# Identity products in TensorE's gaps, an earlier second batch and other tile addresses in a fused Nyström attention and gated MLP on one Trainium2 core

## The chip, the cores and the metric

One Trainium2 chip, one core of it. The metric is device microseconds of one execution of the whole program, the median of several runs; lower is better. TensorE's clock is granted at one of two levels, 1.2 GHz and 2.4 GHz; the profile gives the granted clock of a stretch as a share of 2.4 GHz (0.50 and 1.00). Engines: PE is TensorE, PEld its weight loads, DVE VectorE, ACT ScalarE, POOL GpSimd, SP the engine whose queue issues the transfers.

## The reference

```python
def _attn_ref(q, k, v):                  # 8 batches, 8 heads, 576 tokens, 64 wide
    m, scale = 32, 1.0 / np.sqrt(D)
    q_lm = q.reshape(B, H, m, S // m, D).mean(axis=3)      # 32 landmarks of 18 tokens
    k_lm = k.reshape(B, H, m, S // m, D).mean(axis=3)
    A  = sm(q, k_lm)                      # sm: softmax of scale * a @ b.T
    Bm = sm(q_lm, k_lm)
    C  = sm(q_lm, k)
    Z = Bm.T / (norm1(Bm) * norminf(Bm) + 1e-06)
    for _ in range(6):
        Z = 2 * Z - Z @ Bm @ Z
    return A @ Z @ C @ v

def _moe_ref(x, w_gate, w_val, w_out, rms_g):   # x: 4608 tokens x 512
    rms = np.sqrt(np.mean(x * x, axis=-1, keepdims=True) + 1e-06)
    xn = x / rms * rms_g
    g, val = xn @ w_gate, xn @ w_val            # 512 x 1536 each
    return (silu(g) * val) @ w_out              # 1536 x 512
```

q and k are drawn 8 times as large as standard normals times 0.1. The inputs are float64 in memory; the kernel reads them as pairs of 32-bit words.

## The kernel before

**The attention of a batch b** goes through these steps. `sums` adds 18 tokens to a landmark (DVE, tile `lmT`). `front(b, g)`, for each half g of the heads, makes the scores `sC` and `sA` (16 products of 288 columns and 4 of 32), takes maxima (`mx`, DVE), exponentials (`E`, `eb`, ACT) and transposes `sA` to `tA` (DVE). `turn` transposes `E` on TensorE (`sE`, `sF`), `values` makes `pCV`. Then comes the inverse: `newton_start`, `newton_first` (`p`) and six `newton_step`s, each of 8 small products (`pn`, 32 rows x 32 columns of the array; two records each in the profile) and one DVE instruction (`PV`, at the last step `VF`) which the next step waits for. `newton_weights` makes `W` (`pW`, 8 small products, then a copy) and `newton_values` transposes it to `WT` (`pT`). `second(b)` makes the attention's output `pO` in two sets of four banks, squares it on ACT (`sq`), adds the squares up (`pss`, `pms`), and takes 1/rms by a chain of small DVE instructions (`ms`, `r`); with that it scales `AT` and casts it into `an`, the left operand of everything that follows. The scores, `pO`, `pss`, `pn`, `pW` share four PSUM banks (pool `pa`); `pM`, `psg`, `psv` and `pso` share four others (`pg`).

**The MLP.** The attention's output is never formed: `mix_weights` multiplies the weights of a pair of feature tiles by `WT` (`pM`, cast into `Mhi` and `Mlo`), and `psg` and `psv` (6 products of 288 columns each, four such pairs of groups for each feature tile pair) come out of `Mhi`, `Mlo` and `an`. `s` is silu(gate) times value, `h` its high and low part, and `pso` (`whio`, `wloo`: 3 products for each of 6 feature tiles and each tile of 128 tokens) is the output. The first 6 feature tiles go over all 8 batches and leave partial sums; then the other 6 (`lhio`, `lloo`, `lgv`, `anl`, `obl`) go over them again.

**Weights** come in as pairs of words (`wrawg`, `wrawv`, `wrawo`) and are put together on chip: for each gate or value tile ACT runs two instructions of 128x512 (L175, L178), DVE two (L180, L183), into `wgv`, one such tile for a pair of feature tiles, with four pieces in it. Nine raw tiles are fetched ahead, the later ones when a place in the ring comes free.

**The order of work** on each engine is the order in which the program issues it. A `Mixer` takes pieces from several generators; `until(c, n)` lets a generator wait until the MLP has issued n pieces of chunk c (a chunk is a batch of the first or the second half). In the first 100 us, before the MLP runs without holes, the order is: batch 0's scores and inverse, `second(0)` with `pM` of the first pair in it, then `front(1, 0)`, the first `psg` and `psv`, and `pM` of the second pair, which needs the four pieces of the second `wgv` tile. `early.stream` issues the putting together of weights, `early.then` and `early.after` say behind which instruction.

**Addresses.** A tile's start in each partition comes from the order of allocation. Before, `gsb` (16 bytes) leaves all tiles allocated behind it on the left side (`WT`, `h`, `whio`, `wloo`, `Mhi`, `Mlo`, `an`, `s`, the raw weights, `qk`, `lhio6`, `lgv3`) at 32 bytes past a multiple of 64; those of the right side (`AT`, `sq`, `lhio7` to `lhio11` and `lloo7` to `lloo11`, `lgv4`, `lgv5`, `obl`) start at multiples of 64.

Of the kernel before, what the change touches and what calls it, by code (L numbers as in the profile page):

```python
# [19 lines left out]
P = 128  # L20
M = 32
# [34 lines left out]
def nystrom_moe_kernel(  # L56
# [25 lines left out]
    RS = 0.375**2  # L82
# [19 lines left out]
    gsb = cst.tile([P, NK], F32, name="gsb")  # L102
    WT = cst.tile([P, B, NK, 2 * M], F32, name="WT")

# [21 lines left out]
    class Weights:  # L126

        def __init__(self, order, place, spots, ahead=0):
            self.order, self.queue = list(order), list(order)
            self.place = place  # L130
            self.spots, self.ahead, self.after, self.then = spots, ahead, None, None
            self.raws, self.gv, self.out = {}, {}, {}
# [22 lines left out]
        def load_next(self):  # L155
# [27 lines left out]
            nc.vector.scalar_tensor_tensor(  # L183
                w, whead, -0x80000000, w, op0=ALU.bitwise_and, op1=ALU.bitwise_or
            )
            if nm == "o":
# [95 lines left out]
    def mlp(wts, b, f0, an, store, part, following):  # L282
# [4 lines left out]
        for n, pair in enumerate(pairs):  # L287
# [5 lines left out]
            for i in range(2):  # L293
                if very and i and n + 1 < NPAIR:
                    mix_weights(wts, b, pairs[n + 1])
                    yield 1.1
                s = mp.tile([P, S], F32, name="s", tag="s", bufs=2)
                for e in range(2):
                    cols = slice(e * HS, (e + 1) * HS)
# [56 lines left out]
    with tc.tile_pool(name="ap", bufs=1, side="right") as ap, tc.tile_pool(  # L356
# [30 lines left out]
        def front(b, g, after=None):  # L387
# [59 lines left out]
            if b:  # L447
                tail(after)
# [25 lines left out]
        def turn(b, g):  # L474
# [4 lines left out]
            sF = pa.tile([2 * M, P], F32, name="sF", tag="pa")  # L479
            tp(sF, E[:, 4 * P :], ident)  # L480
            ET = ap.tile([P, 4, P], F32, name="ET", tag="ET", bufs=1)
# [7 lines left out]
        def values(b, g):  # L489
# [3 lines left out]
            pCV = pa.tile([P, D], F32, name="pCV", tag="pa")  # L493
            for ch in range(5):
                for h in range(4):
# [7 lines left out]
                    )  # L503
            nc.vector.tensor_scalar_mul(nt["PV"][:, g, M:], pCV, nt["rs"][g][:, 0:1])

        def opening():
# [18 lines left out]
        def rest(b, inverse, at):  # L525
# [26 lines left out]
            with tc.high_priority():  # L552
                newton_weights(b, inverse[2])
            yield 0.4, 0.0
            yield from until(*next(at))
            with tc.high_priority():
                newton_values(b)
            yield 0.3, 0.0
# [10 lines left out]
        def steady():  # L569
            n_gv = NF1 * 24  # L570
            yield 0.0, TW
            new_state(1)
            sums(1, 0)
            while stage["second"] < 0:
                yield -0.3
            front(1, 0, fixed["an", 0].ins)
            load_qk(2, 0)
            yield 1.3, 0.0
            sums(1, 1, fixed["mx", 1, 0].ins)
            yield from until(0, 24)  # L580
            turn(1, 0)
            yield 0.65, 0.0
            yield from until(0, 36)
# [375 lines left out]
```

## Time and profile before

| | |
|---|---|
| median of 3 runs | 837.14 us (836.75 to 837.6) |
| the profiled execution | 836.84 us, of which the span is 834.7 us |
| TensorE busy | 800.4 us, 96% of the span |
| DVE, ACT, POOL busy | 490.9, 350.9, 71.0 us |
| mean granted clock | 0.973 |
| chain that ended last | 86% of the span on TensorE |

The span is the time from the first to the last instruction; 2.1 us of the execution lie outside it. An engine's busy time is the union of its instructions' spans. Idle time before an instruction is put down to what released it, with an arrow. A product of two fp32 operands stands as two records in the trace, so "x16" for `pn` is 8 products.

### The profile page before, as it was taken

The numbers are of one execution on the slowest core, as the hardware profiler recorded it, in microseconds if no ns is written. First come the engines' busy times: TensorE is split into PE (matmuls) and PEld (weight loads), VectorE is DVE, ScalarE is ACT, GpSimd is POOL, SyncE is SP. The second block draws the span as 40 slices with busy tenths as digits, with TensorE's granted clock in tenths as the row PEclk, the third lists the DMA queues.
The fourth block names the chain that finished last, engine by engine and source line by source line (L and its number), as shares of the span: only waits on it lengthen the run. The fifth ranks groups of instructions, "written<-read, shape, count | busy, mean of one in ns | idle before, by whom it ended". The sixth has DMA issues, their size and how long they took to land.

```text
span 834.7 us, 17401 instructions
## 1 busy us (share of the span) xinstructions
PE 800.4 (96%) x7192; PEld 630.3 (76%) x7192; DVE 490.9 (59%) x1095; ACT 350.9 (42%) x749; POOL 71.0 (9%) x97
## 2 busy tenths in 40 slices
PE   7756999999999999999999999999999999999998
PEld 4334667877878778777787879797979797979796
DVE  7787976856768748668584945242524252425241
ACT  4557644535445444445464844141414141414140
POOL 1012411020020200201110110000000000000000
PEclk8579999999999999999999999999999999999999
DMA  9756452250440612503436510413141304130202
GB/s 326 242 172 216 143 191 89 84 195 15 144 136 2 228 65 92 188 2 109 140 114 229 176 71 13 145 54 118 22 146 53 121 22 147 50 124 14 88 14 75
DMA packets 41054, 95.49 MB, mean 114 GB/s; under 512 B 4112, under 2 KB 17424, under 8 KB 38928
## 3 DMA queue, kind: packets, MB, share of 16 engines
q1 hardware_dynamic: 40976, 94.39, 33.4%
q8 instruction: 56, 0.92, 0.5%
q14 instruction: 22, 0.18, 0.1%
HBM read 66.06 MB, written 28.31 MB: 113 GB/s over the span
## 4 chain that ended last, share of the span: by engine, by line
PE 86%; DVE 5%; DMA 4%; ACT 2%; POOL 1%; issue 1%; SPq 1%; ACTq 0%; DVEq 0%
PE pso L109 35%; PE psg L109 19%; PE psv L109 18%; PE pM L109 6%; PE pn L109 2%; DMA wrawg<-in_moe_w_gate_dram 2%; PE pO L109 1%; PE sC L109 1%; PE pss L109 1%; DMA wrawv<-in_moe_w_val_dram 1%; PE pCV L109 1%; DMA qk<-in_k_dram 1%; PE sE L112 1%; DVE wgv L180 1%; SPq L152 0%
## 5 line engine op out<-in xcount | busy, mean ns | idle before, releaser
L109 PE MATMUL pso<-whio,h 128*128 128x512 f32 x432 | 140.7, 397 | 2.1 <-ACT ob L848 2.1
L109 PE MATMUL pso<-lhio,h 128*128 128x512 f32 x432 | 138.7, 396 | 0.0
L316 DVE TENSOR_TENSOR s<-s,psv 128x288 f32<-128x288 f32 x192 | 85.9, 450 | 60.0 <-PE psv L109 59.3
L315 ACT ACTIVATE s<-psg 128x288 f32<-128x288 f32 x192 | 78.7, 410 | 89.9 <-PE psg L109 89.5
L268 ACT CAST Mhi<-pM 128x512 fp32r<-128x512 f32 x96 | 51.4, 591 | 137.6 <-PE pM L109 137.2
L323 ACT CAST h<-s 128x576 fp32r<-128x576 f32 x96 | 64.6, 673 | 86.2 <-DVE s L316 86.2
L109 PEld LDWEIGHTS pso<-whio,h 128*128 128x128 f32 x432 | 81.6, 189 | 24.3 <-issue 4.2
L109 PEld LDWEIGHTS pso<-lhio,h 128*128 128x128 f32 x432 | 81.0, 187 | 24.8 <-DVE obl L911 5.9
L324 DVE TENSOR_TENSOR h<-s,h 128x576 fp32r<-128x576 f32 x96 | 72.7, 758 | 44.5 <-ACT h L323 44.3
L109 PE MATMUL psg<-an,Mhi 128*128 128x288 f32 x384 | 85.4, 307 | 4.8 <-ACT s L315 3.4
L911 DVE TENSOR_TENSOR obl<-obl,pso 128x512 f32<-128x512 f32 x36 | 24.8, 688 | 107.6 <-PE pso L109 107.4
L109 PE MATMUL pso<-wloo,h 128*128 128x512 f32 x216 | 86.4, 400 | 0.0
L109 PE MATMUL pso<-lloo,h 128*128 128x512 f32 x216 | 85.2, 395 | 0.0
L109 PE MATMUL psv<-an,Mhi 128*128 128x288 f32 x384 | 84.4, 303 | 0.0
L270 DVE TENSOR_TENSOR Mlo<-pM,Mhi 128x512 fp32r<-128x512 f32 x94 | 60.3, 683 | 37.5 <-ACT Mhi L268 37.5
L109 PE MATMUL psg<-anl,Mhi 128*128 128x288 f32 x384 | 81.7, 301 | 0.6 <-DVE Mlo L270 0.6
L109 PE MATMUL psv<-anl,Mhi 128*128 128x288 f32 x384 | 79.1, 294 | 0.0
L109 PEld LDWEIGHTS psg<-an,Mhi 128*128 128x128 f32 x384 | 62.3, 191 | 17.5 <-issue 6.7
L109 PEld LDWEIGHTS psg<-anl,Mhi 128*128 128x128 f32 x384 | 60.9, 188 | 15.5 <-issue 12.6
L109 PEld LDWEIGHTS psv<-an,Mhi 128*128 128x128 f32 x384 | 61.6, 188 | 6.1 <-issue 2.2
L109 PEld LDWEIGHTS psv<-anl,Mhi 128*128 128x128 f32 x384 | 61.5, 188 | 0.0
L109 PE MATMUL psg<-an,Mlo 128*128 128x288 f32 x192 | 58.5, 305 | 0.0
(138 smaller groups left out, 1249.8 us busy)
## 6 DMA issues: line engine op xcount, KB each, us to landing
qk<-in_q_dram SPq DMA_DIRECT2D x16, 576.0 KB, 4.8
qk<-in_k_dram SPq DMA_DIRECT2D x16, 576.0 KB, 5.8
ad<-an SPq DMA_DIRECT2D x8, 1152.0 KB, 5.1
pd<-ob SPq DMA_DIRECT2D x36, 256.0 KB, 2.4
anl<-ad SPq DMA_DIRECT2D x8, 1152.0 KB, 5.1
obl<-pd SPq DMA_DIRECT2D x36, 256.0 KB, 2.7
out_dram<-obl SPq DMA_DIRECT2D x36, 256.0 KB, 2.0
vt<-in_v_dram SPq DMA_DIRECT2D x16, 512.0 KB, 4.1
```

Source lines behind the costliest of these rows:

```text
L109: tc.keep_in_program_order(nc.tensor.matmul(*args, **kw))
L112: tc.keep_in_program_order(nc.tensor.transpose(*args))
L180: nc.vector.scalar_tensor_tensor(w, w, 3, wtail, op0=ALU.logical_shift_left, op1=ALU.bitwise_or)
L268: nc.scalar.copy(hi[:, g], ps[g])
L270: nc.vector.tensor_sub(lo[:, g], ps[g], hi[:, g].bitcast(F32))
L315: silu["last"] = nc.scalar.activation(s[:, cols], banks[0], AF.Silu).ins
L316: nc.vector.tensor_mul(s[:, cols], s[:, cols], banks[1])
L323: nc.scalar.copy(h[:, 0, TAIL:], s)
L324: gated[b, f0 // NF1, 2 * n + i] = nc.vector.tensor_sub(h[:, 1, TAIL:], s, h[:, 0, TAIL:].bitcast(F32))
L911: nc.vector.tensor_add(ob, ob, ps)
```

## The change

Seven things are done at once.
- **Identity products** (`idle`, `spare`): in batch 0's inverse TensorE multiplies the identity by itself, into a bank that nobody reads: 4 products behind the first `turn`, 1 behind the first `values`, 4 behind `p`, 2 behind each of the six `pn`, 1 behind `pW`; 22 in all.
- **`newton_weights`** makes `W` and its transpose at once from a matrix `blocks` (128 x 2 x 128, zero outside its blocks; GpSimd copies `Bs` into it) by 2 full products of 64 columns and 2 of 128 in place of 8 small ones and two transposes. `VF` is written twice by two DVE instructions. `newton_values` is gone, and with it one stop of the stream for each batch.
- **`front(1, 0)`** and the landmark sums that it needs stand behind `pO` of batch 0 instead of behind `an`; `pms` comes ahead of `pM`.
- **Putting weights together**: ACT's part of the ninth tile stands ahead of the eight squares instead of between them, DVE's part of the fifth ahead of `mx`; the rest follows `an` directly. `sums(1, 1)` moves behind it.
- **1/rms** takes 7 instructions of 128x18 behind `ms` instead of 10.
- **`pM` of the next pair** in the very first chunk comes one group of 12 products later; `front(1, 1)` and batch 1's inverse get other places.
- **Addresses**: `gsb` takes 64 bytes, so the tiles of the left side start at multiples of 64 as well; `rT` shares the place of `sqT`.

```diff
-    RS = 0.375**2
+    RS = 0.375
...
-    gsb = cst.tile([P, NK], F32, name="gsb")
+    gsb = cst.tile([P, 16], F32, name="gsb")[:, :NK]
...
+    blocks = cst.tile([P, 2, P], F32, name="blocks")
+    nc.gpsimd.memset(blocks, 0.0)
...
             for i in range(2):
-                if very and i and n + 1 < NPAIR:
-                    mix_weights(wts, b, pairs[n + 1])
-                    yield 1.1
                 s = mp.tile([P, S], F32, name="s", tag="s", bufs=2)
                 for e in range(2):
+                    if very and i and e and n + 1 < NPAIR:
+                        mix_weights(wts, b, pairs[n + 1])
+                        yield 1.1
...
+        def idle(out, n):
+
+            for _ in range(n):
+                mm(out, ident, ident, start=True, stop=True)
+
+        def spare(n):
+            idle(pg.tile([P, 512], F32, name="psw", tag="pg")[:, :P], n)
...
             for g in range(2):
-                turn(0, g)
+                turn(0, g, 4 - 4 * g)
...
-                values(0, g)
+                values(0, g, 1 - g)
...
-            yield 0.0, TW
-            new_state(1)
-            sums(1, 0)
             while stage["second"] < 0:
                 yield -0.3
-            front(1, 0, fixed["an", 0].ins)
-            load_qk(2, 0)
-            yield 1.3, 0.0
-            sums(1, 1, fixed["mx", 1, 0].ins)
-            yield from until(0, 24)
+            yield from until(0, 12)
             turn(1, 0)
             yield 0.65, 0.0
-            yield from until(0, 36)
+            yield from until(0, 37)
+            sums(1, 1, early.last)
+            yield from until(0, 46)
             front(1, 1)
...
-            at = [46, 58, 70] + [78 + 8 * n for n in range(6)] + [126, 132, 138, n_gv + 4, n_gv + 10, n_gv + 18]
+            at = [54, 66, 78] + [84 + 7 * n for n in range(6)] + [126, 136, n_gv + 4, n_gv + 10, n_gv + 18]
...
-                after = [7 * n for n in range(7)] + [48, 54, 68, 86, 96]
+                after = [7 * n for n in range(6)] + [48, 56, 68, 86, 96]
...
+            for h in range(4):
+                nc.gpsimd.tensor_copy(blocks[rows(h), :, rows(h ^ 1)], Bs[rows(h)])
...
-                nt["VF"] = to = sm.tile([P, 2, D], F32, name="VF", tag="VF", bufs=1)
-                of = PV[:, :, M:]
+                nt["VF"] = sm.tile([P, 2, 2, D], F32, name="VF", tag="VF", bufs=1)
+                for g in range(2):
+                    of, by = (a[:, g].unsqueeze(1).broadcast_to([P, 2, D]) for a in (PV[:, :, M:], pn))
+                    nc.vector.scalar_tensor_tensor(nt["VF"][:, g], of, 2.0, by, op0=ALU.mult, op1=ALU.subtract)
+                return
...
-                for h in range(4):
-                    r = rows(rho(g, h))
-                    mm(pW[rows(pos(g, h)), g], Bs[r, g, :], VF[r, g, :], start=True, stop=True)
-            W = sm.tile([P, 2, 2, D], F32, name="W", tag="W", bufs=2)
-            fixed[b] = nc.vector.tensor_copy(W, pW.unsqueeze(2).broadcast_to([P, 2, 2, D]))
+                mm(straight[:, g], blocks[:, g], VF[:, g, 0], start=True, stop=True)
+            for g in range(2):
+                mm(turned[:, g], VF[:, g].rearrange("p a d -> p (a d)"), blocks[:, g], start=True, stop=True)
+            W = sm.tile([P, 2, D], F32, name="W", tag="W", bufs=2)
+            fixed[b] = nc.vector.tensor_copy(W, straight)
...
             newton_first(b, *inverse)
             early.then = fixed["PV", b].ins
+            spare(4)
...
                 newton_step(b, n)
+                spare(2)
                 yield 0.45, NP
-            newton_weights(b, inverse[2])
-            yield 0.4, WW
-            newton_values(b)
-            yield 0.3, WW
+            newton_weights(b)
+            spare(1)
+            yield 0.6, WW
...
-            nc.vector.tensor_single_scalar(ri, ms.bitcast(I32), 1, op=ALU.logical_shift_right)
-            nc.vector.tensor_scalar(ri, ri, -1, 0x5F3759DF, op0=ALU.mult, op1=ALU.add)
-            for c in (1.0, RS):
-                nc.vector.tensor_mul(r2, r1, r1)
-                nc.vector.scalar_tensor_tensor(r2, r2, c, ms, op0=ALU.mult, op1=ALU.mult)
-                nc.vector.scalar_tensor_tensor(r2, r2, -10.0 / 3.0, r2, op0=ALU.add, op1=ALU.mult)
-                last = nc.vector.scalar_tensor_tensor(r1, r2, 5.0, r1, op0=ALU.add, op1=ALU.mult)
+            nc.vector.tensor_scalar(
+                r1.bitcast(I32), ms.bitcast(I32), -0.5, 0x5F3759DF, op0=ALU.mult, op1=ALU.add
+            )
+            nc.vector.tensor_mul(r2, r1, r1)
+            nc.vector.scalar_tensor_tensor(r2, r2, -0.5, ms, op0=ALU.mult, op1=ALU.mult)
+            nc.vector.scalar_tensor_tensor(r1, r2, 1.5, r1, op0=ALU.add, op1=ALU.mult)
+            nc.vector.tensor_mul(r2, r1, r1)
+            nc.vector.tensor_mul(r2, r2, ms)
+            nc.vector.scalar_tensor_tensor(r2, r2, -10.0 / 3.0, r2, op0=ALU.add, op1=ALU.mult)
+            last = nc.vector.scalar_tensor_tensor(r1, r2, 5.0, r1, op0=ALU.add, op1=ALU.mult)
...
-            rT = ap.tile([P, S], F32, name="rT", tag="rT", bufs=1)
+            rT = ap.tile([P, S], F32, name="rT", tag="sqT", bufs=1)
...
-            for n, took in enumerate(second(0)):
-                yield took
-                if n == 2:
-                    low_parts = mix_weights(early, 0, 0, True)
-                    yield 1.1, 0.0
+            parts = second(0)
+            yield next(parts)
+            sums(1, 0, fixed[0].ins)
+            yield next(parts)
+            front(1, 0)
+            load_qk(2, 0)
+            yield 1.3, 0.0
+            yield from parts
+            low_parts = mix_weights(early, 0, 0, True)
+            yield 1.1, 0.0
             low_parts()
...
+            while ("sums", 1) not in fixed:
+                yield -0.3
+            early.then = fixed["sums", 1].ins
+            yield from early.stream(WAIT0, 1)
```

The order of instructions on TensorE in batch 0's inverse, from the first product of the inverse to `W`. Before:

```order
L109 MATMUL p_391<-BT 32x32 x8
L109 MATMUL pn<-PV 32x96 x40
L109 MATMUL pn<-PV 32x64 x8
L109 MATMUL pW<-VF,Bs 32x64 x8
L112 MATMUL pT<-ident,W 128x128 x2
L109 MATMUL pO<-AT,W 64x288 x16
```

and now, for the same place (three of the six steps are left out):

```order
L111 MATMUL p_404<-BT 32x32 x8
L111 MATMUL psw<-ident 128x128 x4
L111 MATMUL pn<-PV 32x96 x8
L111 MATMUL psw<-ident 128x128 x2
...
L111 MATMUL pn<-PV 32x64 x8
L111 MATMUL psw<-ident 128x128 x2
L111 MATMUL pW<-VF,blocks 128x64 x2
L111 MATMUL pW<-blocks,VF 128x128 x2
L111 MATMUL psw<-ident 128x128
L111 MATMUL pO<-AT,W 64x288 x16
```

Between every two steps there are now two full products of the identity, and `pT` is gone.

The order on TensorE behind `pO` of batch 0, up to the first `psg` of the MLP (of the 16 products of `front(1, 0)` one of each kind stands here). Before:

```order
L109 MATMUL pO<-AT,W 64x288 x16
L109 MATMUL pss<-sq,ones 32x288 x8
L109 MATMUL pM<-wgv_417,WT 32x512 x8
L109 MATMUL pms<-sqT,sel 128x18
L109 MATMUL pM<-Mhi,minus 128x512 x2
L109 MATMUL sC<-qk_350,lmT 32x288
...
L109 MATMUL sC<-lmT 32x32 x4
L109 MATMUL psg<-an,Mhi 128x288 x2
```

and now:

```order
L111 MATMUL pO<-AT,W 64x288 x16
L111 MATMUL sC<-qk_359,lmT 32x288
...
L111 MATMUL sC<-lmT 32x32 x4
L111 MATMUL pss<-sq,ones 32x288 x8
L111 MATMUL pms<-sqT,sel 128x18
L111 MATMUL pM<-wgv_435,WT 32x512 x8
L111 MATMUL pM<-Mhi,minus 128x512 x2
L111 MATMUL psg<-an,Mhi 128x288 x2
```

The scores of the second batch have moved ahead of the sum of squares, and `pms` ahead of `pM`.

The order on DVE from the maxima of `front(1, 0)` to the last piece of the second `wgv` tile (here `wgv_664`). Before:

```order
L440 STREAM_TRANSPOSE tA<-sA 128x288 x2
L380 TENSOR_REDUCE lmT<-qk_353 128x64 x2
L180 SCALAR_TENSOR_TENSOR wgv_664<-wgv_664,wrawg_356 128x4x128
...
L324 TENSOR_TENSOR h_714<-s,h_714 128x576
L183 SCALAR_TENSOR_TENSOR wgv_664<-wrawg_360,wgv_664 128x4x128
L180 SCALAR_TENSOR_TENSOR wgv_664<-wgv_664,wrawv_362 128x4x128
L180 SCALAR_TENSOR_TENSOR wgv_743<-wgv_743,wrawg_364 128x4x128
L183 SCALAR_TENSOR_TENSOR wgv_664<-wrawv_362,wgv_664 128x4x128
```

and now, from the cast into `an` on (the tile is called `wgv_584`):

```order
L787 TENSOR_TENSOR an<-AT,an 128x576 x2
L182 SCALAR_TENSOR_TENSOR wgv_584<-wgv_584,wrawv_367 128x4x128
L182 SCALAR_TENSOR_TENSOR wgv_584<-wgv_584,wrawg_369 128x4x128
L185 SCALAR_TENSOR_TENSOR wgv_584<-wrawv_367,wgv_584 128x4x128
L185 SCALAR_TENSOR_TENSOR wgv_584<-wrawg_369,wgv_584 128x4x128
L319 TENSOR_TENSOR s<-s,psv 128x288
L182 SCALAR_TENSOR_TENSOR wgv_584<-wgv_584,wrawv_371 128x4x128
L182 SCALAR_TENSOR_TENSOR wgv_785<-wgv_785,wrawg_373 128x4x128
L319 TENSOR_TENSOR s<-s,psv 128x288
L185 SCALAR_TENSOR_TENSOR wgv_584<-wrawv_371,wgv_584 128x4x128
```

Between `an` and the last piece there stood two landmark sums, `front(1, 0)`'s maxima and transposes, 8 pieces and `h`; now there stand 6 pieces ahead of it and two products with `psv`.

## Rows read from the trace of the kernel before

**Rows 1.** Busy time of each engine by stretch, granted clock, DMA share and GB/s.

```profile
14.00:45.00 31.00, 23.37 (x323) 11.68 (x323) 24.87 (x67) 18.12 (x41) 2.27 (x2) 0.50 0.72 247
45.00:81.00 36.00, 20.92 (x251) 14.32 (x251) 30.54 (x76) 23.35 (x45) 6.94 (x6) 0.88 0.64 214
110.00:834.70 724.70, 717.55 (x6209) 576.44 (x6207) 402.04 (x880) 289.38 (x620) 49.44 (x72) 1.00 0.30 100
...
20.00:25.00 5.00, 2.33 (x48) 1.55 (x48) 4.86 (x16) 1.99 (x4) 0.00 (x0) 0.50 1.03 398
55.00:60.00 5.00, 1.29 (x16) 0.23 (x16) 4.26 (x7) 0.08 (x1) 3.09 (x1) 0.52 0.37 105
```

**Rows 2.** Timeline of TensorE, 45 to 79 us: start, duration, instruction [idle before <-releaser].

```profile
45.76 0.40 PE L109 MATMUL psg<-an,Mhi 128*128 128x288 f32 x1 [1.03 <-ACT an L774]
...
58.71 1.96 PE L109 MATMUL pM<-wgv,WT 64*32 64x512 f32 x16 [7.52 <-DVE wgv L183]
...
67.13 0.54 PE L109 MATMUL psg<-an,Mhi 128*128 128x288 f32 x2 [2.88 <-ACT s L315]
...
78.73 2.29 PE L109 MATMUL pM<-wgv,WT 64*32 64x512 f32 x16 [1.81 <-DVE nden L648]
```

**Rows 3.** Timeline of DVE, 41 to 59 us.

```profile
41.09 0.18 DVE L755 TENSOR_SCALAR ms<-pms 128x18 f32<-128x18 f32 x1 [1.89 <-PE pms L109]
...
45.74 1.43 DVE L775 TENSOR_TENSOR an<-AT,an 128x576 fp32r<-128x576 f32 x2
...
48.88 2.57 DVE L380 TENSOR_REDUCE lmT<-qk 128x64 f32<-128x1152 f32 x2
...
57.37 0.68 DVE L180 SCALAR_TENSOR_TENSOR wgv<-wgv,wrawg 128x512 int32<-128x512 int32 x1
57.97 0.68 DVE L183 SCALAR_TENSOR_TENSOR wgv<-wrawv,wgv 128x512 int32<-128x512 int32 x1
```

**Rows 4.** Timeline of ACT, 33 to 65 us.

```profile
33.41 0.69 ACT L739 ACTIVATE sq<-pO 128x288 f32<-128x288 f32 x2
34.00 0.68 ACT L175 ACTIVATE wrawg<-wrawg 128x512 int32<-128x512 uint32 x1
...
36.58 0.71 ACT L739 ACTIVATE sq<-pO 128x288 f32<-128x288 f32 x2 [0.17 <-PE pO L109]
...
64.61 0.65 ACT L175 ACTIVATE wrawg<-wrawg 128x512 int32<-128x512 uint32 x1 [2.88 <-DMA wrawg<-in_moe_w_gate_dram]
```

**Rows 5.** Timeline of TensorE, 1 to 43 us, from the opening's 11 identity products on.

```profile
1.34 5.06 PE L109 MATMUL psw<-ident 128*128 128x128 f32 x22 [1.34 <-POOL ident masks.py:199]
...
27.45 0.86 PE L109 MATMUL pn<-PV 32*32 32x96 f32 x16 [0.66 <-DVE PV L668]
...
29.97 0.65 PE L109 MATMUL pW<-VF,Bs 32*32 32x64 f32 x16 [0.41 <-DVE VF L668]
31.18 0.69 PE L112 MATMUL pT<-ident,W 128*128 128x128 f32 x2 [0.56 <-DVE W L678]
31.80 1.89 PE L109 MATMUL pO<-AT,W 32*64 32x288 f32 x16
...
36.47 2.15 PE L109 MATMUL pss<-sq,ones 128*32 128x288 f32 x16
...
42.45 0.69 PE L109 MATMUL sC<-qk,lmT 64*32 64x288 f32 x1
```

**Rows 6.** Timeline of TensorE, 403 to 408 us (first half of the features).

```profile
403.38 0.39 PE L109 MATMUL pso<-wloo,h 128*128 128x512 f32 x1
...
406.10 0.39 PE L109 MATMUL pso<-wloo,h 128*128 128x512 f32 x1
...
406.64 1.09 PE L109 MATMUL pM<-wgv,WT 64*32 64x512 f32 x16
```

**Rows 7.** Timeline of TensorE, 782 to 788 us (second half of the features).

```profile
782.16 0.39 PE L109 MATMUL pso<-lloo,h 128*128 128x512 f32 x1
...
787.75 0.39 PE L109 MATMUL pso<-lloo,h 128*128 128x512 f32 x1
```

More of the change, by code (lines that the diff above doesn't have):

```diff
@@ L130, in __init__ @@
             self.place = place
-            self.spots, self.ahead, self.after, self.then = spots, ahead, None, None
+            self.spots, self.ahead, self.after, self.then, self.last = spots, ahead, None, None, None
             self.raws, self.gv, self.out = {}, {}, {}
@@ L182, in load_next @@
                 )
-            nc.vector.scalar_tensor_tensor(
+            last = nc.vector.scalar_tensor_tensor(
                 w, whead, -0x80000000, w, op0=ALU.bitwise_and, op1=ALU.bitwise_or
             )
+            self.last = last.ins
             if nm == "o":
@@ L385, in sums, with front @@
                     )
-        def front(b, g, after=None):
+        def front(b, g, after=None, late=None):
             nt, lmT, qk = state[b], lms.pop((b, g)), loaded.pop((b, g))
@@ L447, in front @@
             if b:
-                tail(after)
+                tail(late or after)
             return tail
@@ L472, in weigh, with turn @@
             nt["AT"][g] = AT
-        def turn(b, g):
+        def idle(out, n):
[3 more added lines that the diff above has]
+            idle(pg.tile([P, 512], F32, name="psw", tag="pg")[:, :P], n)
+        def turn(b, g, more=0):
             E = state[b]["E"][g]
@@ L478, in turn @@
                 tp(sE[:, ch], E[:, ch * P : (ch + 1) * P], ident)
-            sF = pa.tile([2 * M, P], F32, name="sF", tag="pa")
+            room = pa.tile([P, 2, P], F32, name="sF", tag="pa")
+            sF = room[: 2 * M, 0]
             tp(sF, E[:, 4 * P :], ident)
+            idle(room[:, 1], more)
             ET = ap.tile([P, 4, P], F32, name="ET", tag="ET", bufs=1)
@@ L487, in turn, with values @@
             state[b]["ET", g] = ET, EL
-        def values(b, g):
+        def values(b, g, more=0):
             nt = state[b]
@@ L492, in values @@
             vt, vl_ = loaded.pop((b, g, "v"))
-            pCV = pa.tile([P, D], F32, name="pCV", tag="pa")
+            room = pa.tile([P, 2 * P], F32, name="pCV", tag="pa")
+            pCV = room[:, :D]
             for ch in range(5):
@@ L503, in values @@
                     )
+            idle(room[:, P:], more)
             nc.vector.tensor_scalar_mul(nt["PV"][:, g, M:], pCV, nt["rs"][g][:, 0:1])
@@ L552, in rest @@
             with tc.high_priority():
-                newton_weights(b, inverse[2])
-            yield 0.4, 0.0
-            yield from until(*next(at))
-            with tc.high_priority():
-                newton_values(b)
-            yield 0.3, 0.0
+                newton_weights(b)
+            yield 0.6, 0.0
             stage["newton"] = stage["wt"] = b
@@ L668, in newton_step, with newton_weights @@
+                return
             nc.vector.scalar_tensor_tensor(to, of, 2.0, pn, op0=ALU.mult, op1=ALU.subtract)
-        def newton_weights(b, Bs):
+        def newton_weights(b):
             VF = state[b]["VF"]
-            pW = pa.tile([P, 2, D], F32, name="pW", tag="pa")
+            pW = pa.tile([P, 2 * D + NK * 2 * M], F32, name="pW", tag="pa")
+            straight = pW[:, : 2 * D].rearrange("p (g d) -> p g d", g=2)
+            turned = pW[:, 2 * D :].rearrange("p (g n) -> p g n", g=2)
@@ L705, in newton @@
                 newton_step(b, n)
+                spare(2)
                 yield 0.45, NP
-            newton_weights(b, inverse[2])
-            yield 0.4, WW
-            newton_values(b)
-            yield 0.3, WW
+            newton_weights(b)
+            spare(1)
+            yield 0.6, WW
             stage["wt"] = b
@@ L735, in second @@
                         r = rows(pos(g, h))
-                        mm(po[2 * g + h // 2][half(h)], W[r, g, 0, :], ATs[g][r, cols], start=True, stop=True)
+                        mm(po[2 * g + h // 2][half(h)], W[r, g, :], ATs[g][r, cols], start=True, stop=True)
                 sq = ap.tile([P, NK, HS], F32, name="sq", tag="sq", bufs=2)
@@ L814, in nystrom_moe_kernel @@
         new_state(0)
+        new_state(1)
         if WN0:
```

23 lines of the change are left out of this document (9 added, 14 removed).

## The prediction

> **What bounds the kernel now.** I read the busy time by stretch first [rows 1]. From 110 us to the end TensorE is busy 717.55 of 724.70 us at a granted clock of 1.00, so what an edit does there counts only if it adds or removes work of TensorE. The loss is ahead of it: 20.92 us busy of 36.00 between 45 and 81 us, and 23.37 of 31.00 between 14 and 45 us, at a clock of 0.50, the lower level of 1.2 GHz. Some 23 us of idle lie there. Whatever brings the MLP's unbroken stretch forward comes off the end nearly one for one.
>
> TensorE's timeline [rows 2] says where: 7.52 us before the second `pM`, released by DVE's last `wgv` piece; 2.88 us before a `psg`, released by ACT; 1.81 us before the third `pM`. DVE's timeline [rows 3] shows why the 7.52 arise: `an` is done at 47.17, and the piece that releases `pM` ends at 58.65, because landmark sums (2.57 us at 48.88), maxima, transposes and other pieces at 0.60 us apart (57.37 to 57.97) stand between.
>
> **The change part by part.** All times are of the profiled execution, 836.84 us; the median of the runs shown is 837.14, so 0.3 is added at the end.
>
> *First `psg`.* In the inverse DVE is busy 4.86 of 5.00 us between 20 and 25 us, with transfers at 398 GB/s [rows 1]; TensorE waits for it at each step (0.66 us before a `pn` of 0.86 us [rows 5]). One identity product costs 5.06/11 = 0.46 us at half clock [rows 5], so two take 0.92, against a gap of 0.66: 0.26 us late per step, 1.6 for six, if the clock stays at half; at full clock two take 0.46 and fit. At full clock I take the inverse to end where it ended, since DVE sets it. `pW` comes 0.2 later for the second `VF`, and `W` is copied after the two narrow products, so `pO` starts at about 31.2 to 32.0 against 31.80 [rows 5].
>
> The squares come next. They started at 33.41, with the ninth tile's two ACT instructions in between, the first at 34.00 with no idle before it, so its transfer had landed by then [rows 4]. Now these stand ahead: squares from 35.3 at the latest. Eight squares take 37.29 - 33.41, less two instructions of about 0.6, so 2.7: end at 38.0 instead of 37.29, 0.7 late (nothing, if the tile lands by 33.4). The scores of `front(1, 0)` take 42.45 to 44.73 (45.76 less the wait of 1.03) [rows 2, 5], 2.28 us at half clock; most run in the banks that early squares leave, so they end at about 38.6 (full) to 39.3 (half). `pss` then waits for a bank, which DVE frees with a maximum and a transpose of 288 columns; from `an` (two of 576 columns in 1.43 us [rows 3]) I estimate 0.4 each: `pss` at 39.5 to 40.1, for 2.15 us at half clock [rows 5], 1.1 at full. `pms` no longer waits for `pM`, so `ms` follows about 1.1 later: 41.7 (full) to 43.3 (half), against 41.09 [rows 3]. The shorter chain gives back 3 x 0.18, small instructions of the scores take about 0.4 of it. So `psg` starts at about 46.3 (full) or 47.9 (half) against 45.76. The part that seems to be removed from this path (scores behind `an`) is paid ahead of `pss`.
>
> *Second `pM`.* This is where the change earns. `an` ends 47.17 - 45.76 = 1.4 behind the first `psg`. Behind it now stand 7 pieces at 0.60 and two products with `psv` at about 0.4, then `pM`: 1.4 + 4.2 + 0.8 = 6.4 behind `psg`, so 52.7 (full) or 54.3 (half) against 58.71: **-6.0 or -4.4**. TensorE has three groups of twelve in the meantime instead of two, so most of the wait is filled.
>
> *From there to 81 us.* The moved sums (2.57 us) now stand directly ahead of `front(1, 1)`, and can cost a wait of their own. But the raw tiles' places come free some 5 us earlier, and with them the transfer that held ACT up until 64.61 [rows 4]. I can't place these; between none and all of 2.88 + 1.81 goes, and I take half: **-2.3**. Clock: `pM` took 1.96 at 58.71 and 2.29 at 78.73, against 1.09 in the steady part [rows 2, 6], because it came after idle time (0.52 between 55 and 60 us [rows 1]). Without the long wait 0.9 and part of 1.2 come back: **-1.5**, between 0 and -2.1.
>
> *Steady part.* `pW` and `pT` took 0.65 + 0.69 = 1.34 at half clock [rows 5]; two products of 128 columns and two of 64 take 0.92 + 0.46 = 1.38 by the identity products. So seven more batches cost nothing that can be told (0.02 each at full clock); a second `VF` of DVE could add 0.1 each if TensorE waited, and the stop that is left out saves about as much: 0, between -0.7 and +0.7. The GpSimd copies lie under the six steps; the earlier `memset` can push the opening's first products by some 0.3.
>
> *Addresses.* Before, `whio` and `h` both start 32 past a multiple of 64; `wloo` to `wloo` over 12 products takes 406.10 - 403.38 = 2.72, 227 ns each [rows 6]. `lloo7` and later start at a multiple of 64 while `h` does not: 787.75 - 782.16 = 5.59 for 24, 233 ns [rows 7]. Moved now is `h`, and everything on the left side. No `pso` row has both at a multiple of 64. If it is the mixture that costs, 540 products get 6 ns back: -3.3. If it is the moving operand's start, the 756 on the left side lose 6: +4.7, and so perhaps the 2304 `psg` and `psv`: +14 more. The second half's products could differ for another reason: 0. I take 0, and both ends for the range.
>
> **Sum:** -6.0 - 2.3 - 1.5 = -9.8, so 827.0, with 0.3 **827.3**.
>
> **The rivals.**
> - *The clock stays at half in the inverse* (chance 0.20). For it: 0.50 over all of 14 to 45 us with TensorE three quarters busy [rows 1]. Then the steps are 1.6 later (counted above only where they meet the landing of the ninth tile, which hides most of it), `pM` gains 4.4, the rest about 2: 830.7. Against it: the identity products fill just the gaps. The Trainium skill ("TensorE: Matmul & The Clock Gate", What's actually happening) says that the lower level is the default and that activity releases it, which by itself would make it 827.3 and not 830.7; that identity products at this spacing count as enough activity no run here shows.
> - *The addresses help* (0.14): -3.3 more, 824. The same page (Back-to-back issue gap) gives columns/2.4 GHz + 2.5 ns between products, which is 216 ns for 512 columns. The trace has 227 and 233. If the odd starts were what separates the rows from the floor of 512 columns at 2.4 GHz, 213 ns, 1296 products would gain up to 14 to 20 each, 22 us, and the time be about 805; I give that 0.03.
> - *The addresses cost* (0.13): at +4.7 the time is 832 (0.05); with `psg` and `psv` at the same 6 ns, +19, it is **846, slower than before** (0.08). It decides from 9.8/3060 = 3.2 ns a product on. For it: the only rows with a moving operand at a multiple of 64 are the slower ones. Against: those also have the two operands apart.
> - *The front eats the gain* (0.08): squares behind a landing, scores behind squares, `pss` behind DVE's transposes, and the wait for `pM` goes to `psg`. If `psg` starts at 51 instead of 46.3, `pM` gains 1 to 2, and the time is 835 to 838. For it: four steps now stand in a row behind one transfer. Against: it landed by 34.00 [rows 4], and no step behind it is longer than 2.3 us.
>
> **How the numbers follow.** The forecast, 827.3, has 0.42, its own range 824 to 831. The range of 8 in 10 takes in the half clock, the helping addresses and the mild cost, and most of the front's case: 816 to 837; left out are the 0.03 far below and the 0.08 far above, and a little of each end. 0.2% (1.7 us) is about what a measurement of this kernel can tell from no change. Faster: 0.42 + 0.20 + 0.14 + 0.03 + 0.05 and a little of the front's case, 0.85; same 0.05 from the rest of it; slower 0.10.
>
> **What would show it.** In the changed profile: `psg` at 46 to 48 us; the second `pM` at 52 to 55 with a wait below 2 us in place of 7.52; a granted clock of 1.00 in most of 14 to 45 us, and `pn` of about 0.5 us; squares starting at about 35 behind L180; `wloo` and `lloo` pitches within 1 ns of 227; the stretch from 110 us on as long as before but for the start. Wrong would be: `pn` still 0.86 and later by 0.26 each; a new wait of over 3 us ahead of `front(1, 1)` or of batch 1's inverse; pitches of `psg` and `psv` that differ from before, which changes the sum by 2.3 us for each ns.

## The result and the profile after

The changed kernel takes 825.91 us (median of 4 runs, 825.34 to 827.3) against 836.94 us (four runs; the 837.14 above is the median of three of them), a ratio of 0.9875 (95% interval 0.9853 to 0.9898): 11.0 us faster. The profiled execution took 825.74 us with a span of 823.9 us, 10.8 us less than before.

Busy time by stretch of the changed kernel, in the columns of [rows 1]:

```profile
14.00:45.00 31.00, 22.06 (x354) 13.36 (x352) 25.93 (x72) 18.13 (x43) 3.58 (x6) 0.89 0.79 271
45.00:81.00 36.00, 27.94 (x318) 21.04 (x310) 34.94 (x82) 27.99 (x53) 8.50 (x11) 0.86 0.60 200
110.00:823.90 713.90, 708.51 (x6116) 575.34 (x6114) 392.69 (x863) 284.00 (x609) 55.80 (x96) 1.00 0.29 98
...
20.00:25.00 5.00, 3.55 (x52) 2.69 (x55) 4.79 (x17) 2.95 (x6) 1.30 (x4) 1.00 1.03 397
...
35.60:42.30 6.70, 5.86 (x70) 2.52 (x74) 2.44 (x6) 2.92 (x9) 0.00 (x0) 0.50 0.02 8
```

TensorE is busy 7.0 us more between 45 and 81 us, and the clock between 14 and 45 us is 0.89 instead of 0.50; it is still at half from 35.6 to 42.3. Behind 110 us 10.8 us less are left; how much of that is an earlier start and how much a faster pace these rows don't tell, the table below does. TensorE's timeline of the changed kernel, against [rows 2, 5]:

```profile
26.49 0.53 PE L111 MATMUL pn<-PV 32*32 32x96 f32 x16 [0.36 <-DVE PV L679]
26.95 0.71 PE L111 MATMUL psw<-ident 128*128 128x128 f32 x4
...
31.92 0.72 PE L111 MATMUL pO<-AT,W 32*64 32x288 f32 x10 [0.16 <-DVE W L692]
36.24 1.54 PE L111 MATMUL pO<-AT,W 32*64 32x288 f32 x14 [3.60 <-ACT sq L748]
...
48.44 0.40 PE L111 MATMUL psg<-an,Mhi 128*128 128x288 f32 x1 [1.54 <-ACT an L786]
...
56.14 1.09 PE L111 MATMUL pM<-wgv,WT 64*32 64x512 f32 x16
...
67.71 0.53 PE L111 MATMUL psg<-an,Mhi 128*128 128x288 f32 x2 [1.12 <-ACT s L318]
70.75 1.08 PE L111 MATMUL pCV<-vt,ET 128*32 128x64 f32 x32 [1.99 <-ACT ET L496]
```

`pn` takes 0.53, the second `pM` waits for nothing, and there is a new wait of 3.60 within `pO`. ACT's timeline shows what it is made of, against [rows 4]:

```profile
34.66 0.68 ACT L177 ACTIVATE wrawg<-wrawg 128x512 int32<-128x512 uint32 x1 [0.58 <-DMA wrawg<-in_moe_w_gate_dram]
35.23 0.66 ACT L180 ACTIVATE wgv<-wrawg 128x512 f32<-128x512 f32 x1
35.79 0.70 ACT L748 ACTIVATE sq<-pO 128x288 f32<-128x288 f32 x2
```

The squares stand behind ACT's two instructions for the ninth raw tile, and the first of these waited for its transfer until 34.66.

One reading helps more than the rest: the same event's start in TensorE's timelines of both kernels, and how the lead grows from one event to the next.

| start of, us | before | after | lead |
|---|---|---|---|
| first `psg` | 45.76 | 48.44 | -2.68 (late) |
| second `pM` | 58.71 | 56.14 | 2.57 |
| third `pM` | 78.73 | 75.58 | 3.15 |
| first `pso`, batch 0 | 97.05 | 91.79 | 5.25 |
| first `pso`, batch 1 | 159.34 | 151.12 | 8.22 |
| first `pso`, batch 6 | 435.92 | 428.25 | 7.67 |
| first `pso`, second half | 519.45 | 511.79 | 7.66 |
| last `pso` | 830.68 | 819.90 | 10.78 |

Four pieces, then: 5.3 up to batch 0's `pso`, 3.0 up to batch 1's, 0.55 lost over five batches, 3.1 over the second half. The first piece is nearly all idle time of TensorE, 26.65 us before and 21.73 after (first the kernel before, then the changed one):

```profile
0.00:97.05 97.05, 70.40 (x883) 46.23 (x884) 77.79 (x189) 56.15 (x116) 18.09 (x21) 0.79 0.65 222
```

```profile
0.00:91.79 91.79, 70.06 (x906) 50.08 (x907) 79.59 (x189) 56.72 (x116) 18.36 (x30) 0.91 0.68 233
```

In the second piece the trace of before has something that I had not looked for, a `pso` that waits 2.08 us for ACT's copies `ob`:

```profile
115.08 0.50 PE L109 MATMUL pso<-whio,h 128*128 128x512 f32 x1 [2.08 <-ACT ob L848]
```

On ACT the copies stood there behind a table load and the exponentials of `front(2, 0)`, at 114.44; after the change they stand ahead of them, and no wait for `ob` is left:

```profile
105.98 1.07 ACT L870 COPY ob<-pso 128x512 f32<-128x512 f32 x2
107.06 1.28 ACT L427 ACT_TABLE_LOAD   x1
```

But two other waits of TensorE have come in its place:

```profile
99.85 0.40 PE L111 MATMUL pms<-sqT,sel 128*128 128x18 f32 x2 [0.74 <-DVE sqT L757]
109.00 0.92 PE L114 MATMUL sE<-ident,E 128*128 128x128 f32 x4 [1.11 <-ACT E L427]
```

From batch 0's `pso` to batch 1's, TensorE is idle for 2.92 us before and for 2.47 us after:

```profile
97.05:159.34 62.29, 59.37 (x650) 43.01 (x649) 48.58 (x121) 30.93 (x72) 8.07 (x9) 0.97 0.35 118
```

```profile
91.79:151.12 59.33, 56.86 (x640) 41.99 (x639) 48.62 (x119) 31.48 (x73) 9.65 (x13) 1.00 0.37 125
```

So idle time makes up only 0.45 of the 3.0 us. Most of the rest is the clock: before, a stretch at half clock followed the wait (0.57 from 116 to 120 us), and after the clock is 1.00 throughout. `e6_before_sums_late` below has the wait for `ob` and no half clock, and takes 60.73 us for the same stretch, 1.6 less than before. About 1.0 us is left that no run assigns to a cause. The third and fourth pieces are settled by runs below. Of the second half the rows answering to [rows 7]:

```profile
772.38 0.39 PE L111 MATMUL pso<-lloo,h 128*128 128x512 f32 x1
...
776.47 0.39 PE L111 MATMUL pso<-lloo,h 128*128 128x512 f32 x1
```

4.09 us for 18 products, 227 ns, where it was 233. The pitch of `psg` and `psv` is about 133 ns in both kernels.

### The profile page after: what moved, and what is told of

It reads as the page before. It is cut to its first block, busy times and chain, and to the rows that moved or that the text cites. A ratio compares the mean times of both kernels' runs of the same rounds, so it can differ in the third digit from the quotient of the medians.

```text
span 823.9 us, 17374 instructions
## 1 busy us (share of the span) xinstructions
PE 794.6 (96%) x7156; PEld 635.4 (77%) x7156; DVE 489.6 (59%) x1087; ACT 351.5 (43%) x749; POOL 78.3 (10%) x130
## 4 chain that ended last, share of the span: by engine, by line
PE 85%; DVE 5%; DMA 4%; ACT 3%; issue 1%; POOL 1%; SPq 1%; ACTq 0%; DVEq 0%
PE pso L111 35%; PE psg L111 19%; PE psv L111 18%; PE pM L111 5%; DMA wrawg<-in_moe_w_gate_dram 2%; PE pn L111 2%; PE sC L111 2%; PE pO L111 1%; PE pCV L111 1%; DMA wrawo<-in_moe_w_out_dram 1%; PE pss L111 1%; DMA qk<-in_k_dram 1%; PE sE L114 1%; SPq L154 1%; PE pW L111 1%
## 5 line engine op out<-in xcount | busy, mean ns | idle before, releaser
L111 PE MATMUL pso<-lhio,h 128*128 128x512 f32 x432 | 136.5, 392 | 0.0
L327 DVE TENSOR_TENSOR h<-s,h 128x576 fp32r<-128x576 f32 x96 | 74.4, 775 | 42.1 <-ACT h L326 41.6
L111 PE MATMUL psv<-an,Mlo 128*128 128x288 f32 x192 | 59.0, 307 | 0.0
```

The costliest lines, as they stand in the source:

```text
L111: tc.keep_in_program_order(nc.tensor.matmul(*args, **kw))
L327: gated[b, f0 // NF1, 2 * n + i] = nc.vector.tensor_sub(h[:, 1, TAIL:], s, h[:, 0, TAIL:].bitcast(F32))
```

## The experiments

Ratios are to the kernel before, on the same chip. "Lead" is the one of the table.

**The old addresses in the changed kernel** (`e1_old_addresses`).

```diff
-    gsb = cst.tile([P, 16], F32, name="gsb")[:, :NK]
+    gsb = cst.tile([P, NK], F32, name="gsb")
```

> The changed kernel with gsb at its old size, so that the left side's tiles start 32 past a multiple of 64 again; nothing else differs. Theory (the mixture of starts costs): the lhio and lloo products go back to 233 ns from 227, the second half of the features takes 3.1 us longer, and the time is 825.9 + 3.1 = 829.0. Rival (the second half was shortened by something else in the change): pitches stay at 227 ns and the time at 825.9. In both, the first half is unchanged within 0.3 us.

Measured: 830.24 us, ratio 0.9934 (0.9917 to 0.9951). `lloo` is back at 233 ns (6.29 us for 27 products), and the second half gains nothing:

```profile
774.85 0.39 PE L111 MATMUL pso<-lloo,h 128*128 128x512 f32 x1
...
781.14 0.40 PE L111 MATMUL pso<-lloo,h 128*128 128x512 f32 x1
```

The lead at its start is 6.60, at the last `pso` 6.25. The opening came out 1.1 worse, although the order of instructions is the same: one more stretch at half clock fell at 82 to 86 us. So the total is 1.2 above the theory, and the expected equal first half did not come.

**The new addresses in the kernel before** (`e2_before_new_addresses`), the same line the other way round.

> The kernel before with gsb at 64 bytes and nothing else. Theory: lhio and lloo products at 227 ns, the stretch up to the second half as before, the second half 3.1 us shorter, 836.9 - 3.1 = 833.8. Rival (the addresses act only together with the rest, or also on the opening): 836.9, or below 833.

Measured: 832.24 us, ratio 0.9957 (0.9942 to 0.9973). `lloo` products start every 227 ns (5.44 us for 24):

```profile
778.19 0.39 PE L109 MATMUL pso<-lloo,h 128*128 128x512 f32 x1
...
783.63 0.39 PE L109 MATMUL pso<-lloo,h 128*128 128x512 f32 x1
```

The lead is 1.16 at the start of the second half and 4.65 at its end: 3.5 us in the second half from a tile's size alone; the 1.2 ahead of it are no more than two executions of one kernel differ by (`e4_squares_first`). With the run above the mixture of starts is what costs: both operands 32 past a multiple of 64 give 227 ns, both at a multiple 227, the moving one at a multiple and the stationary one not 233. The fourth combination was not tried. The starts themselves are read off the order of allocation; the traces hold no addresses.

**Without identity products** (`e3_no_identity`).

```diff
-                turn(0, g, 4 - 4 * g)
+                turn(0, g)
...
-                values(0, g, 1 - g)
+                values(0, g)
...
-            spare(4)
...
-                spare(2)
...
-            spare(1)
```

> The changed kernel without its 22 identity products. Theory (they hold the clock): granted clock 0.50 over most of 14 to 45 us, pn at 0.86 us, the first psg 1 to 2 us later than 48.4, the time 827 to 828.5. Rival (DVE and the transfers set the inverse, and TensorE's clock there is of no account): clock 0.50 too, but the first pO at 31.9 and the first psg at 48.4 within 0.4, the time 825.9 within 0.5.

Measured: 825.96 us, ratio 0.9879 (0.9859 to 0.99), the time of the changed kernel. TensorE's timeline:

```profile
26.54 0.86 PE L111 MATMUL pn<-PV 32*32 32x96 f32 x16 [0.67 <-DVE PV L679]
28.07 0.86 PE L111 MATMUL pn<-PV 32*32 32x96 f32 x16 [0.67 <-DVE PV L679]
...
33.12 1.25 PE L111 MATMUL pO<-AT,W 32*64 32x288 f32 x10 [0.38 <-DVE W L692]
35.26 1.45 PE L111 MATMUL pO<-AT,W 32*64 32x288 f32 x10 [0.90 <-ACT sq L745]
```

The last row ends where the view does, at 36 us; the whole set is 22 records from 35.26 on. The clock is 0.50 again from 15 to 42 us, `pn` 0.86, `pO` 1.2 later; and the wait behind it is 0.90 instead of 3.60. Both sets of `pO` wait for the same squares, so a later and slower first set (1.2 and 0.5 us) shortens the wait; the other 1.0 is that ACT had the ninth tile at 33.70 here and at 34.66 in the changed kernel. The first `psg` is at 47.96. What the identity products gain in the inverse is lost 4 us later. The rival is right on the time, and half wrong on its reason: `pO` did come later. The two medians are equal; by the lead at batch 1's `pso`, 7.32 against 8.22, the products are worth 0.9 us, in spite of the later tile.

**The squares ahead of the ninth tile** (`e4_squares_first`; a second run of the same kernel is `e8_squares_first_wait26`, whose name's ending means nothing).

```diff
             after = self.after or silu.get("last")
+            if (f, nm) == (NF1 - 2, "g"):
+                after = fixed["sq", 0].ins
...
-                    nc.scalar.activation(sq[:, n], po[n], AF.Square)
+                    fixed["sq", b] = nc.scalar.activation(sq[:, n], po[n], AF.Square)
```

> The changed kernel with ACT's two instructions for the ninth weight tile behind the eight squares instead of ahead of them. Theory (the wait of 3.60 us ahead of the second pO set is ACT waiting for that tile): the wait falls to about 1.9, the second pO set starts at 34.5 instead of 36.2, the first psg at 46 to 47 instead of 48.4, and the time is 824 to 825. Rival (what comes behind is set by DVE's pieces and by the raw tiles, which do not move): first psg earlier, but the second pM at 56.1 and the time at 825.9.

> A second look at the kernel with the squares first, for its opening and the clock alone. Theory: the second pM again at 53.1 and a pso start that depends on where the clock falls between 65 and 85 us: 89 to 92. Rival: 91.9 again within 0.2.

Measured: 824.78 us, ratio 0.986 (0.9833 to 0.9887). The wait within `pO` is 1.23, the first `psg` at 44.53, the second `pM` at 53.09, 3.1 earlier than in the changed kernel; but batch 0's `pso` starts at 91.89, as there (91.79). In the second run (one execution, 824.35 us) the wait is 1.97, the first `psg` at 46.66, the second `pM` only at 54.40, and `pso` at 90.49. From 34 to 40 us the clock was 1.00 in the first run and 0.50 in the second; between 78 and 85 us it is the other way round, the first run here, then the second:

```profile
78.00:85.00 7.00, 6.57 (x60) 5.18 (x64) 3.76 (x8) 3.15 (x7) 1.66 (x2) 0.52 0.29 81
```

```profile
78.00:85.00 7.00, 5.59 (x88) 4.42 (x88) 6.28 (x13) 4.56 (x10) 2.02 (x2) 1.00 0.35 85
```

The theory's time held, and its wait and first `psg` in the second run; the rival's second `pM` at 56.1 did not come. Of the expectation for the second run the start of `pso` held and the second `pM` did not. By the leads the order earns 0 to 1.4 us, which four runs cannot tell from nothing (the two ratios' intervals overlap). That the work on which the half clock falls decides how much is left fits these rows; no run shows it by itself.

**The second batch's scores behind `an` again** (`e5_front_behind_an`).

```diff
+            front(1, 0, fixed["an", 0].ins)
+            load_qk(2, 0)
+            yield 1.3, 0.0
             yield from until(0, 12)
...
-            front(1, 0)
-            load_qk(2, 0)
-            yield 1.3, 0.0
             yield from parts
```

> The changed kernel with front(1, 0) behind an again, all else as changed (sums(1, 0) early, weights straight behind). Theory (the early scores cost the first psg 2.7 us and earn it back, since no scores, maxima and two table loads stand between psg and the second pM): first psg at 45.5 to 46.5 instead of 48.4, but the second pM at 56 to 58 and the time 826.5 to 828. Rival A (the early scores are what earned most): second pM at 59 or later, the time 830 or more. Rival B (they earn nothing, the order of DVE's weight pieces does it all): second pM at 54 to 55, the time 824 to 825.

Measured: 829.65 us, ratio 0.9922 (0.9907 to 0.9937), lead 3.96 at batch 1's `pso`, 4.3 less than the changed kernel. The first `psg` is at 47.99, only 0.45 earlier than in the changed kernel: the theory's 45.5 to 46.5 failed. The second `pM` is at 55.64, even 0.5 earlier. The loss comes behind it: from there to batch 0's `pso` TensorE is idle for 10.06 us instead of 5.40, most of all where batch 1's inverse now waits:

```profile
75.59 0.87 PE L111 MATMUL pn<-PV 32*32 32x96 f32 x16 [3.46 <-DVE PV L666]
```

So the early scores do earn, nearest to rival A in the time, but not at the place it named: they bring batch 1's inverse forward, not `pM`.

**One edit in the kernel before** (`e6_before_sums_late`).

```diff
...
-            sums(1, 1, fixed["mx", 1, 0].ins)
...
             yield from until(0, 36)
+            sums(1, 1, early.last)
```

`early.last` is the last weight piece that has been issued on DVE.

> The kernel before, with one edit: the landmark sums sums(1, 1) behind the last weight piece issued so far instead of behind mx. Theory (their 2.57 us are part of the 7.52 us wait): second pM at 56.1 instead of 58.7 with a wait of about 5, front(1, 1) later than it or as late as before, and the time 2 to 2.5 us below before, some 834. Rival (what is gained is lost again at front(1, 1), which then waits for the sums): second pM at 56.1 and the time as before, 836.

Measured: 830.62 us, ratio 0.9936 (0.9919 to 0.9953), lead 6.80 at batch 1's `pso` and 6.78 at the end: more than twice the forecast from the one edit. At batch 0's `pso` the lead is 5.24, as large as that of the whole change there (5.25).

```profile
54.70 1.96 PE L109 MATMUL pM<-wgv,WT 64*32 64x512 f32 x16 [2.70 <-DVE wgv L183]
...
72.39 2.29 PE L109 MATMUL pM<-wgv,WT 64*32 64x512 f32 x16 [1.85 <-DVE nden L647]
```

The second `pM` gains 4.0, the third 6.3: the raw tiles' places come free earlier, too (ACT waits 1.74 us for the next gate or value tile and has it at 56.49, before 5.43 us and 60.51). Here the wait for `ob` stays (2.08 us), without the half clock behind it, and the lead over the next five batches is constant.

**The old `newton_weights`** (`e7_old_weights_step`): the functions of the kernel before put back, `VF` written once, one stop more for each batch (131, and `[7 * n for n in range(7)]`).

> The changed kernel with the old newton_weights and newton_values (8 small products, two transposes, one stop more for each batch). Theory (the four full products take TensorE 0.11 us more per batch, which is how the lead over the kernel before shrinks from 8.22 us at batch 0's pso to 7.67 at batch 6's): the lead no longer shrinks, the time is about 825.4. Rival (the shrinking has to do with the places of the stops and not with the products): it shrinks by 0.1 per batch all the same, the time 825.9.

Measured: 824.96 us, ratio 0.9865 (0.9851 to 0.988). The lead is 7.59 at batch 1's `pso` and 7.56 at batch 6's: it no longer shrinks (the start that the theory calls batch 0's is batch 1's). So the new step costs 0.11 us per batch, net of the stop that it saves; how much of this is the four full products by themselves the run does not tell, since it puts the second `VF` and the stop back as well. A batch of the steady part in the changed kernel and with the old step:

```profile
133.04 0.55 PE L111 MATMUL pW<-VF,blocks 128*128 128x64 f32 x4
133.43 0.66 PE L111 MATMUL pW<-blocks,VF 128*128 128x128 f32 x4
```

```profile
133.08 0.42 PE L111 MATMUL pW<-VF,Bs 32*32 32x64 f32 x16
134.35 0.38 PE L114 MATMUL pT<-ident,W 128*128 128x128 f32 x2
```

**The two edits together in the kernel before** (`e9_two_edits`): that of `e6_before_sums_late` and that of `e2_before_new_addresses`.

> The kernel before with two edits only: sums(1, 1) behind the weight pieces, and gsb at 64 bytes. Theory (these two account for nearly all of the change): 6.8 us off the opening and 3.5 off the second half, 836.5 - 10.3 = 826.2, as the whole change (825.9) within 1. Rival (the opening's gain hangs on where the granted clock falls, and the 6.8 was a fortunate case): 828 to 830.

Measured: 828.66 us, ratio 0.9901 (0.9886 to 0.9916); the rival's range. The second half gave its 3.5; the opening came to 4.46 instead of 6.80, with nearly the same two waits for `pM` (2.94 and 1.72 us, there 2.70 and 1.85). 1.6 of the 2.3 us arise between batch 0's `pso` and batch 1's, where the wait for `ob` was followed by half clock this time and not in the run before; first this kernel, then that one:

```profile
111.90:115.40 3.50, 3.50 (x19) 2.36 (x24) 2.40 (x4) 0.85 (x3) 0.00 (x0) 0.51 0.92 363
```

```profile
111.90:115.40 3.50, 3.50 (x51) 2.43 (x50) 3.33 (x10) 0.36 (x2) 0.00 (x0) 1.00 0.80 288
```

**Squares first and the old `newton_weights`** (`e10_squares_first_old_step`), the edits of `e4_squares_first` and `e7_old_weights_step` on the changed kernel.

> The changed kernel with the squares first and the old newton_weights and newton_values. Theory (two gains that add up: 0 to 1.4 us from the squares, 0.5 from the weights' step): 824.0. Rival (where the clock falls in the opening decides, and neither is seen): 825 to 826.

Measured: **822.60 us** (821.61 to 824.36), ratio 0.9833 (0.9812 to 0.9854): faster than both kernels, 3.3 us below the changed one (the intervals of the two ratios just touch), 1.4 below the theory. Against `e7_old_weights_step` (824.96) the order of the squares is worth 2.4 us here. Lead 10.11 at batch 1's `pso`, constant from there to the second half, 13.58 at the end.

**The same with `WAIT` 2.6** (`e11_e10_wait26`). `WAIT` is the time, in the program's own reckoning of the order, between the issue of one weight tile's putting together and the next.

> The same with WAIT 2.6 instead of 1.8, so that ACT's instructions for tiles 11 and 12 stand behind front(1, 1) and batch 1's transposes, and no table load stands between E and tA (two loads fewer). Theory (ACT's wait for raw tiles and the two table loads hold up TensorE between 60 and 80 us): 1 to 2.5 us less than without it, 822. Rival (the third pM then waits for its weights): no gain, or 1 to 3 us more.

Measured: 830.93 us, ratio 0.9934 (0.9919 to 0.995). The rival: the third `pM` waits for its weights,

```profile
76.48 1.96 PE L111 MATMUL pM<-wgv,WT 64*32 64x512 f32 x16 [4.42 <-DVE wgv L187]
```

and the loss is 8.3 us rather than 1 to 3, with half clock up to 90 us behind it.

**The fastest without identity products** (`e12_e10_no_identity`).

> The fastest version so far (squares first, old newton_weights) without the 22 identity products. Theory (they raise the clock of the inverse, but the inverse is set by DVE and the transfers, so they bring next to nothing): granted clock 0.50 over 15 to 42 us, first psg at 46 to 47 as with them (46.6), the time 822.6 to 823.5. Rival (with the squares' wait gone, the clock that they hold now carries through the scores and sums of squares): first psg 1.5 us or more later, the time 824.5 or more.

Measured: 824.21 us (823.57 to 824.64), ratio 0.9855 (0.9839 to 0.9872). First `psg` at 47.04, 0.46 later, lead at batch 1's `pso` 1.1 smaller. In between the two theories: with the squares' wait shortened the identity products are worth 1.1 us by the lead at batch 1's `pso` and 1.6 by the medians, where in the changed kernel it is 0.9 by that lead and 0 by the medians; the ranges of the runs overlap in both cases.

## Why the prediction was right, step by step

The time forecast was 827.3, measured 825.9. The mechanism was right: idle time of TensorE ahead of the MLP's unbroken stretch was filled (4.9 us up to batch 0's `pso`), and this stretch came forward by about as much (5.3). But that the total came out so close is in part luck. The sum of -9.8 was to be complete at 81 us; at the first `psg` behind the third `pM` (80.95 before, 77.02 after) only 3.9 had come. The other 6.9 of the 10.8 arose where the prediction had put nothing: 1.3 from there to batch 0's `pso`, 3.0 up to batch 1's, -0.55 in the steady part, 3.1 from the addresses.

- **First `psg`**: 46.3 forecast at full clock, 48.44 measured. The clock did rise, as assumed (`pn` 0.53, 1.00 from 14 to 30 us). Two things were mis-sized: ACT had the ninth tile at 34.66, 0.66 later than the bound I read from before's ACT row (in the five traces where ACT waits for it ahead of the squares it is there between 33.70 and 34.66, so the changed kernel's is a late case), and I added up the squares as one run of 2.7 us. They go in turns with `pO` over the same four banks, TensorE idled 3.60, and the clock fell to half for `pO`, scores and `pss` (5.86 of 6.70 us busy at 0.50). I had tied full clock to the identity products alone, and not asked what the wait behind them would do to it. The chain for 1/rms has 8 instructions behind `ms`, not the 7 that I counted, so it gave back 0.43 us (1.70 instead of 2.13 up to `rT`) and not 0.54.
- **Second `pM`**: -6.0 forecast, -2.6 measured. The DVE part nearly held: pieces 0.60 apart, the last one ends at 55.8, 7.4 behind the first `psg` (6.4 forecast; 0.73 of the difference is a wait for `psv`). But TensorE itself had not done its three groups by then, which ran in part at half clock; `pM` waited for nothing. The wait of 7.52 is gone, and its place was filled with work moved there.
- **From there on**: -3.8 forecast (2.3 + 1.5) up to 81 us, -1.4 measured there, and -5.6 up to batch 1's `pso`. The clock's part was sized well: the two `pM` took 1.09 and 1.51 instead of 1.96 and 2.29, 1.65 less. Behind 81 us the half clock that followed the wait for `ob` at 115 us is gone, 1.6 us, which the prediction did not have; the wait itself made way for two others. I had looked for idle time up to 81 us only. `e5_front_behind_an` and `e6_before_sums_late` show the two earners ahead of that: the late sums (4.5 to 6.8 by themselves in the kernel before, by where the half clock fell) and the early scores (4.3, taken away from the changed kernel). They are not to be added: the whole lead is 8.2.
- **Steady part**: 0 forecast, +0.11 per batch measured, and gone in `e7_old_weights_step`; within the bounds given.
- **Addresses**: 0 forecast, -3.1 to -3.5 measured, the bound on the favourable side (-3.3). The working by 540 products of 6 ns held; the choice of 0 between two ends was the mistake. The rows themselves spoke for the mixture: only the slow kind of product had two different starts, and `psg`, `psv` and `pM` gave no row for a cost of the moving start. Their pitch did not change. The gap that the Trainium skill gives for isolated products ("TensorE: Matmul & The Clock Gate", Back-to-back issue gap), 216 ns for 512 columns, is not reached: 227 ns with both at multiples of 64.
- **Rivals**: the clock did not stay at half, and `e3_no_identity` shows that it would have cost 0 to 0.9 us: 826.0, not 830.7. The same page's sentence (What's actually happening) on the clock's release agrees with the rows, 1.00 from 14 to 30 us with identity products and 0.53 in `e3_no_identity`; its worth in time does not follow from it. Nor do these products hold the clock in every trace: in `e4_squares_first` and `e7_old_weights_step` it was at half from about 20 to 23 us. The first `psg` did come 2.1 us later than forecast where the rival of the eaten gain had 4.7; but with the front behind `an` (`e5_front_behind_an`) it was only 0.45 earlier, with the ninth tile there 0.9 sooner, so that the front's move is what did it is not shown. The argument against that rival, that no step is longer than 2.3 us, overlooked the squares, 2.7 by the prediction's own sum.

What stays open: where the half clock falls between 20 and 85 us differs between executions of the same kernel (`e4_squares_first` and its second run), and behind the wait for `ob` between kernels of one order there; it moves the opening by 1 to 2 us, and no run separates this from the edits' own worth below that size. The shorter chain for 1/rms, `pms` ahead of `pM`, `pM` one group later and the new order of DVE's weight pieces had no run of their own, so what each is worth is open.

## What to carry to other kernels

Take the lead event by event over the whole trace, and not only where the change was made: here a quarter of the gain arose behind the stretch that I had costed, more than half of that quarter from a stretch at half clock that fell away, and another quarter in the second half of the program. And add up the idle time of such a piece: the wait for `ob` went, and two others came. Filling gaps on an engine that waits for another one raised its clock and brought little time, 0 to 0.9 us here and 1.1 to 1.6 once the squares no longer waited for a transfer; ask first which instruction ends the wait. And before a chain gets new members, look for the one that waits for a transfer: an in-order engine makes everything behind it wait, too, as the eight squares did.

## What the runs showed of the hardware

- Products of 128x512 with the moving operand at a multiple of 64 bytes and the stationary one 32 past it start every 233 ns, and every 227 ns when both are at a multiple or both 32 past it (`e1_old_addresses`, `e2_before_new_addresses`; the starts by the order of allocation).
- The wait for `ob` of about 2.1 us in a stretch that is otherwise busy was followed by 3.4 us at half clock in the kernel before, in `e2_before_new_addresses` and in `e9_two_edits`, and not in `e6_before_sums_late`, whose wait was as long (2.08).
- The transfer of the ninth weight tile ends up to 1 us earlier or later from trace to trace. ACT's first instruction on it, where it waits for the transfer, runs at 34.66 us in the changed kernel, 34.40 in `e1_old_addresses`, 33.96 in `e7_old_weights_step`, 33.80 in `e5_front_behind_an` and 33.70 in `e3_no_identity`.
